# Zeros written by VectorE ten units into the third block, attention's steps queued ahead of the gates', and one routing step a unit later

## The chip, the cores and the metric

The kernel runs on one core of one Trainium2 chip. Its time is in device microseconds (us), from the first to the last work of the core; a version's time is the median of its runs. Beside the timed runs there is one profiled execution, from which all rows come.

## What is computed

Three layers follow each other. Attention works on chunks of 64 positions; its output is the input of a dense layer pair with a hard-swish-like gate; that output goes through a mixture of eight experts, of which each token uses the best two.

```python
scores = scale * np.matmul(q_c, k_c.transpose(0, 1, 2, 4, 3))
attn = softmax(scores)                       # within a chunk of 64
x = np.matmul(attn, v_c)                     # as 2304 tokens x 512
h = x @ w_in                                 # 512 -> 2048
x = (h * np.clip(h + 3.0, 0.0, 6.0) / 6.0) @ w_out
noisy_logits = x @ w_gate + np.log1p(np.exp(x @ w_noise)) * noise
top2 = np.argpartition(-noisy_logits, 2, axis=1)[:, :2]
...
out[mask] += top2_w[mask, k, None] * (np.maximum(x[mask] @ w1[e], 0.0) @ w2[e])
```

## The kernel before, in words

The 2304 tokens are 18 tiles of 128 rows, in five blocks of 4, 3, 4, 4 and 3 tiles (BT, lines 31 to 33). The dense layer runs block by block, and each block is 16 units (the 2048 inner columns by 128). A unit of `regular` (line 781) is, on TensorE: 12 matmuls into one bank (`s1`, line 297: four row pieces in three passes, since an operand is split into a high and a low fp32r part), then three matmuls for each tile of the unit before (`s2`, line 307). ScalarE and VectorE turn the bank into the next operand between them (lines 332 to 339), so TensorE is always one unit behind with the second product.

Into these units other work is woven, by `between` (line 802). Three dictionaries, A, B and Z, say what is run at which place of which unit: Z right after `mlp_s1`, A after `mlp_act`, B at the unit's end. A counter (`ticks`) puts TensorE's part between the matmuls of `s1` and `s2`. While block b is worked on:

- attention of the tiles of block b+1 is made: scores (`att_sc`, line 200, TensorE), maximum and difference (lines 207 and 213, VectorE), exponential (line 226, ScalarE), in the next unit the sums and the normalising (`att_n`, lines 231 to 238, VectorE), then transposes (line 250, TensorE), a copy (line 254, ScalarE), the product with v (line 267, TensorE) and the split of the result (lines 277 and 280). At the end the next tile of q, k and v is loaded into the freed half of `arena` (line 122, SP's queue).
- the gates of block b-1 are made. `x2_out` (line 363) stores the four finished tiles of block b-1 in DRAM (`x2d`). `gate_l` (line 383) loads a tile back with its rows turned into quarters, four small loads `xq<-x2d` on SP's queue; `gate_d` (line 375) transposes it on VectorE into `xT`; `gate_mm` (line 415, TensorE) multiplies it with the gate weights, two tiles at a time; `gate_lp`, `gate_rt` and `gate_rr` sum it up.
- `gate_top` (line 446 on) picks the two experts in four steps, `gate_pm` (line 502, TensorE) and `gate_ps` (line 518 on) find each token's slot, and `gate_ps` ends with indirect DMAs from GpSimd's queue that write the table (line 525).

TensorE, VectorE and ScalarE run exactly in the order in which the program calls these steps (`manual_schedule`). SP's and GpSimd's queues do not: a planner puts their instructions where it reckons that their operands are ready. Each engine takes its own instructions strictly one after the other, so an instruction that waits holds all behind it.

`zero_out` (line 739) fills one tile of 128x1024 with zeros (line 741) and writes it with five DMAs of 1536 KB from SP's queue over the first rows of `x2d` and over the whole output (line 745), to which the experts add later. The tile is one of three buffers that carry raw weights elsewhere.

The calls, with their numbers (unit numbers of attention; unit and tiles of a gate; unit of `gate_top`, steps of it in a unit):

```python
regular(1, {}, *between(1, (1, 4, 7, 10), ((4, 2), (8, 2)), 11, 2))
side = {}
at(side, 8, zero_out)
regular(2, side, *between(2, (1, 3, 5, 7), ((4, 2), (8, 1)), 10, 2))
```

After the fourth block the experts follow, eight units each, with gathers from `x2d`, their products and the adding scatters into the output.

Of the kernel before, what the change touches and what calls it, by code (L numbers as in the profile page):

```python
# [19 lines left out]
P = 128  # L20
NT = 2304
DM = 512
# [6 lines left out]
B0 = [sum(BT[:b]) for b in range(len(BT))]  # L29
# [23 lines left out]
def tile_kernel(ctx, tc, qkv, w1u, w2u, wg, noise, out):  # L53
    nc = tc.nc
# [8 lines left out]
    first = tc.tile_pool(name="first", bufs=1, space=PSUM)  # L63
# [13 lines left out]
    def bank(tag, shape, name):  # L77
        i, j = in_pair[tag]
        t = single[tag] if tag in single else pairs[i][:, j * DM:(j + 1) * DM]
        if len(shape) == 2:  # L80
            return t[:, :shape[1]]
        return t[:, :shape[1] * shape[2]].rearrange("p (a b) -> p a b", b=shape[2])
# [235 lines left out]
    def gtile():  # L318
        return work.tile([P, 2 * CAP], F32R, tag="g", bufs=2, name="g")


    def mlp_s1(b, u, g, off):
        n = BT[b] * P
        h = hbank(n)
        s1(h, st["w", "m", u], xb[b], 0, n)
        st["h", b] = h
        st["g", b, u] = g[:, off:off + 2 * n].rearrange("p (j n) -> p j n", j=2)

    def mlp_act(b, u):
        n = BT[b] * P  # L330
        r = work.tile([P, DM], F32, tag="r", bufs=2, name="r")[:, :n]
        nc.scalar.activation(r, st["h", b], AF.Relu, bias=b3)  # L332
        nc.vector.scalar_tensor_tensor(r, r, 6.0, st["h", b], op0=ALU.min, op1=ALU.mult)  # L333
        nc.scalar.activation(st["g", b, u][:, 0], r, AF.Copy)  # L334
        st["r", b] = r

    def mlp_lo(b, u):
        g = st["g", b, u]
        nc.vector.tensor_tensor(g[:, 1], st["r", b], g[:, 0].bitcast(F32), op=ALU.subtract)  # L339

    def mlp_o(b, u):
        if u == 0:
            st["acc", b] = [bank(ACC[i], [P, DM], "acc") for i in range(BT[b])]
        s2(st["acc", b], st.pop(("g", b, u)), st["w", "m", u], BT[b], u == 0, u == U1 - 1)


    def x2_out(b):
        extra = None
        for i in range(BT[b]):
            t = B0[b] + i  # L350
            if b == NB - 2 and i > 2:
                x2 = arena[:, i]
            elif i > 2:
                if extra is None:
                    extra = work.tile([P, 2, DM], F32, tag="raw", bufs=3, name="x2e")
                x2 = extra[:, i % 2]
            else:
                x2 = work.tile([P, DM], F32, tag="x2", bufs=3, name="x2")
            if i % 2 == 1:
                nc.vector.tensor_scalar(x2, st["acc", b][i], 1.0 / 6.0, None, op0=ALU.mult)  # L360
            else:
                nc.scalar.activation(x2, st["acc", b][i], AF.Copy, scale=1.0 / 6.0)
            nc.sync.dma_start(x2d[ND + t * P:ND + (t + 1) * P, :], x2)
            st["x2", t] = x2
# [40 lines left out]
    ENDS = [pairs[0][:, :2 * P], pairs[0][:, 6 * P:]]  # L405
# [332 lines left out]

    def zero_out():
        zero = work.tile([P, 2 * DM], F32, tag="raw", bufs=3, name="zero")  # L740
        nc.gpsimd.memset(zero, 0.0)  # L741
        for d in (x2d[:ND], out):
            d = d.rearrange("(p r) d -> p (r d)", p=P).rearrange("p (r d) -> p r d", d=2 * DM)
            for r in range(0, d.shape[1], 3):
                nc.sync.dma_start(d[:, r:r + 3], zero[:, None, :].to_broadcast([P, 3, 2 * DM]))
# [33 lines left out]
    def at(d, u, f, *a):  # L779
        d.setdefault(u, []).append((f, *a))  # L780

    def run(lst):
        for f, *a in lst:
            f(*a)
# [6 lines left out]
    def regular(b, side, A={}, B={}, Z={}):  # L791
        nonlocal prev
        for u in range(U1):
            mlp_s1(b, u, gtile(), 0)
            run(Z.get(u, []))
            mlp_act(b, u)
            run(A.get(u, []))
            for pb, v in prev:
                mlp_o(pb, v)
            mlp_lo(b, u)  # L800
            for pb, v in prev:
                if v == U1 - 1:
                    x2_out(pb)
            run(B.get(u, []))
            if b == NB - 1 and u > 0:
                pump()
            run(side.get(u, []))
            prev = [(b, u)]

    def between(b, attn, gates, top, per):  # L810


        A, B, Z, nt, n0 = {}, {}, {}, BT[b], st.get("tick", 0)
        before = BT[b - 1]

        def s2_(u, k, f, *a):
            n = n0 + 3 + k if u == 0 else n0 + 3 + before + (3 + nt) * (u - 1) + 3 + k
            at(ticks, n, f, *a)

        def s1_(u, k, f, *a):  # L820
            n = n0 + k if u == 0 else n0 + 3 + before + (3 + nt) * (u - 1) + k
            at(ticks, n, f, *a)


        first = B0[b - 1]
        for u, n in gates:
            ts = list(range(first, first + n))
            first += n
            for i, t in enumerate(ts):
                at(B, u - n - 1 + i, gate_l, t)  # L830
                at(B, u - n + i, gate_d, t)
            if nt > 3:
                s2_(u, nt, gate_mm, ts, ENDS[0])
                at(B, u, gate_lp, ts)
                s1_(u + 1, 2, gate_rt, ts, ENDS[1])
                s1_(u + 1, 2, gate_rr, ts)
            else:
                p5 = bank("p5", [P, DM], "lg")
                s1_(u + 1, 1, gate_mm, ts, p5)
                at(A, u + 1, gate_lp, ts)  # L840
                s1_(u + 2, 1, gate_rt, ts, p5[:, 2 * P:])
                s1_(u + 2, 1, gate_rr, ts)
        for i, u in enumerate(attn):
            t = B0[b + 1] + i
            if nt > 3:
                s2_(u, nt, att_sc, t, 0, outer)
            else:
                s1_(u, 2, att_sc, t, 0, outer)
            at(B, u, att_mx, t, False)
            at(B, u, att_e, t)  # L850
            at(B, u + 1, att_n, t)
            if nt > 3:
                s1_(u + 2, 3, att_pt, t)
                at(A, u + 2, att_at, t, at_[0])
                s2_(u + 2, nt, att_xo, t)
                end = (B, u + 2)
            else:
                s2_(u + 2, 1, att_pt, t)
                at(B, u + 2, att_at, t, at_[0])
                s1_(u + 3, 2, att_xo, t)  # L860
                end = (Z, u + 3)
            at(*end, att_hi, t)
            at(*end, att_lo, t)
            if t + 2 < NTILE:
                at(*end, load_tile, t + 2, bufs[4 + t % 2])
        for i in range(4):
            at(B, top + i // per, gate_top, b - 1, 1)
        pos, pm = ENDS[1] if nt > 3 else bank("p5", [P, DM], "pos"), top + 5 - per
        s2_(pm, 1, gate_pm, b - 1, pos)
        at(B, pm, gate_ps, b - 1)  # L870
        return A, B, Z
# [51 lines left out]
    def pump():  # L923

        j = nxt["u"]
        if j < U1 + NE * U2:
            split_unit(j)
            load_raw(j + 3)
            nxt["u"] = j + 1
# [24 lines left out]

    with tc.manual_schedule(engines={nc.tensor.engine, nc.vector.engine, nc.scalar.engine}):
        block0()
        regular(1, {}, *between(1, (1, 4, 7, 10), ((4, 2), (8, 2)), 11, 2))
        side = {}
        at(side, 8, zero_out)
        regular(2, side, *between(2, (1, 3, 5, 7), ((4, 2), (8, 1)), 10, 2))  # L960
        side = {}
        for j in range(3):
            at(side, 12 + j, load_raw, U1 + j)
        regular(3, side, *between(3, (1, 3, 5), ((4, 2), (8, 2)), 10, 1))
# [5 lines left out]
    side = {}  # L970
# [7 lines left out]
    for gi, (key, e, t0, nt, off) in enumerate(groups):  # L978
        side = {}
# [127 lines left out]
```

## Time and profile before

| | before |
|---|---|
| time, median of 3 runs | 949.82 us (948.93 to 951.11) |
| the profiled execution's own time | 942.81 us |
| its span, first to last instruction | 941.0 us |
| TensorE busy | 909.5 us (97%) |
| VectorE, ScalarE, GpSimd busy | 51%, 35%, 24% |
| mean granted TensorE clock | 0.991 |
| moved by DMA | 101.49 MB |

A line of the grouped view reads: line of the kernel, engine, operation, what it writes and reads, number, then busy us and mean ns, then the idle time of the engine before it and what ended that. In views in order of time the first two numbers are the start and the duration in us, and a bracket at the end gives the idle time of the engine just before and its releaser. PE is TensorE, PEld its weight load, DVE VectorE, ACT ScalarE, POOL GpSimd, SPq the queue of SP.

### The profile page before, as it was taken

The numbers are of one execution on the slowest core, as the hardware profiler recorded it, in microseconds if no ns is written. First come the engines' busy times: TensorE is split into PE (matmuls) and PEld (weight loads), VectorE is DVE, ScalarE is ACT, GpSimd is POOL, SyncE is SP. The second block draws the span as 40 slices with busy tenths as digits, with TensorE's granted clock in tenths as the row PEclk, the third lists the DMA queues.
The fourth block names the chain that finished last, engine by engine and source line by source line (L and its number), as shares of the span: only waits on it lengthen the run. The fifth ranks groups of instructions, "written<-read, shape, count | busy, mean of one in ns | idle before, by whom it ended". The sixth has DMA issues, their size and how long they took to land. (4 is left out here: it accounts for less than half of the span.)

```text
span 941.0 us, 14426 instructions
## 1 busy us (share of the span) xinstructions
PE 909.5 (97%) x5814; PEld 767.7 (82%) x5814; DVE 481.5 (51%) x907; ACT 331.5 (35%) x638; POOL 230.4 (24%) x213
## 2 busy tenths in 40 slices
PE   6999996999999999999999999999999999999996
PEld 3677785887778777888988898888898988888884
DVE  6999962554544454336553455444545544441311
ACT  5555431333332232244551443333333333321210
POOL 0000000002001000032202435753655445332311
PEclk9999997999999999999999999999999999999998
DMA  9636548113220310013640664563636455240422
GB/s 346 204 102 195 187 173 285 38 64 57 79 90 1 112 57 1 1 57 83 187 147 2 161 165 129 125 151 95 158 99 132 118 118 140 69 54 20 54 24 33
DMA packets 49916, 101.49 MB, mean 108 GB/s; under 512 B 17040, under 2 KB 23056, under 8 KB 49840
## 3 DMA queue, kind: packets, MB, share of 16 engines
q1 hardware_dynamic: 38736, 80.38, 27.4%
q0 software_dynamic: 11104, 20.10, 11.8%
q8 instruction: 47, 0.77, 0.4%
q14 instruction: 29, 0.24, 0.1%
HBM read 77.66 MB, written 22.75 MB: 107 GB/s over the span
## 5 line engine op out<-in xcount | busy, mean ns | idle before, releaser
L307 PE MATMUL bp<-w,g 128*128 128x512 f32 (+1 forms) x1812 | 451.1, 396 | 0.4 <-ACT g L334 0.3
L307 PEld LDWEIGHTS bp<-w,g 128*128 128x128 f32 (+1 forms) x1812 | 329.3, 185 | 73.9 <-DVE g L339 0.8
L297 PE MATMUL bp<-Xa,w 128*128 128x304 f32 (+3 forms) x1344 | 244.0, 332 | 2.5 <-ACT w L181 2.1
L297 PEld LDWEIGHTS bp<-Xa,w 128*128 128x128 f32 x1344 | 209.1, 188 | 30.3 <-ACT w L181 5.5
L560 POOL DMA_INDIRECT xrq<-x2d,iq x114 | 119.3, 1046 | 95.9 <-DVE iq L554 34.6
L603 DVE SCALAR_TENSOR_TENSOR g<-bp,g 128x304 fp32r<-128x304 f32 (+2 forms) x128 | 60.3, 471 | 131.0 <-ACT g L602 131.0
L142 DVE TENSOR_TENSOR w<-raw,w 128x1024 fp32r<-128x1024 f32 x64 | 78.4, 1226 | 89.3 <-ACT w L141 87.6
L525 POOL DMA_INDIRECT table<-pay,slot x36 | 36.1, 1002 | 346.6 <-DVE slot L522 245.0
L602 ACT ACTIVATE g<-bp 128x304 fp32r<-128x304 f32 (+2 forms) x128 | 54.2, 424 | 168.7 <-PE bp L297 168.5
L297 PE MATMUL bp<-Xb,w 128*128 128x384 f32 (+1 forms) x480 | 107.0, 368 | 0.0
L297 PE MATMUL bp<-Xe,w 128*128 128x304 f32 (+1 forms) x672 | 102.7, 308 | 0.0
L297 PEld LDWEIGHTS bp<-Xe,w 128*128 128x128 f32 x672 | 99.8, 188 | 3.3
L333 DVE SCALAR_TENSOR_TENSOR r<-r,bp 128x512 f32<-128x512 f32 (+1 forms) x80 | 50.6, 632 | 91.0 <-ACT r L332 90.9
L297 PEld LDWEIGHTS bp<-Xb,w 128*128 128x128 f32 x480 | 86.7, 190 | 11.8 <-issue 1.2
L630 POOL DMA_INDIRECT out_dram<-arena,tab x40 | 62.7, 1566 | 123.6 <-DVE arena L627 100.2
L141 ACT ACTIVATE w<-raw 128x1024 fp32r<-128x1024 f32 x64 | 67.7, 1058 | 59.2 <-PE bp L307 58.6
L332 ACT ACTIVATE r<-bp,b 128x512 f32<-128x512 f32 (+1 forms) x80 | 51.1, 639 | 106.0 <-PE bp L297 106.0
L334 ACT ACTIVATE g<-r 128x512 fp32r<-128x512 f32 (+1 forms) x80 | 47.2, 590 | 73.3 <-DVE r L333 73.3
L339 DVE TENSOR_TENSOR g<-r,g 128x512 fp32r<-128x512 f32 (+1 forms) x80 | 51.0, 637 | 40.2 <-ACT g L334 40.2
L181 ACT ACTIVATE w<-u 128x512 fp32r<-128x512 f32 x32 | 20.3, 633 | 32.8 <-DVE u L174 32.8
L375 DVE STREAM_TRANSPOSE arena<-xrq 128x512 f32<-128x512 f32 (+1 forms) x30 | 31.4, 1045 | 0.0
L741 POOL MEMSET zero<- 128x1024 f32 x1 | 1.0, 953 | 115.3 <-DVE u L174 115.3
(150 smaller groups left out, 478.3 us busy)
## 6 DMA issues: line engine op xcount, KB each, us to landing
raw<-in_w2u_dram SPq DMA_DIRECT2D x64, 512.0 KB
raw<-in_w1u_dram SPq DMA_DIRECT2D x24, 512.0 KB
arena<-in_qkv_dram SPq DMA_DIRECT2D x14, 768.0 KB
out_dram<-zero SPq DMA_DIRECT2D x4, 1536.0 KB
rawx<-in_w1u_dram SPq DMA_DIRECT2D x8, 512.0 KB
x2d<-x SPq DMA_DIRECT2D x15, 256.0 KB
xq<-x2d SPq DMA_DIRECT2D x44, 64.0 KB
xrq<-x2d,iq POOLq DMA_INDIRECT x114, 3.0
```

What stands on the lines that cost most here:

```text
L141: nc.scalar.activation(w[:, 0], raw, AF.Copy)
L142: nc.vector.tensor_tensor(w[:, 1], raw, w[:, 0].bitcast(F32), op=ALU.subtract)
L297: nc.tensor.matmul(dst, w[:, a, kd * P:(kd + 1) * P], x[:, b, kd, t0:t0 + n], start=(k == 0), stop=(k == 3 * KD - 1))
L307: nc.tensor.matmul(acc[i][:gi.shape[2]], gi[:, a], w[:, b, DM:], start=(first and j == 0), stop=(last and j == 2))
L332: nc.scalar.activation(r, st["h", b], AF.Relu, bias=b3)
L333: nc.vector.scalar_tensor_tensor(r, r, 6.0, st["h", b], op0=ALU.min, op1=ALU.mult)
L334: nc.scalar.activation(st["g", b, u][:, 0], r, AF.Copy)
L339: nc.vector.tensor_tensor(g[:, 1], st["r", b], g[:, 0].bitcast(F32), op=ALU.subtract)
L560: nc.gpsimd.indirect_dma_start(out=xr[:, c * P:(c + 1) * P], out_offset=None, in_=x2q, in_offset=bass.IndirectOffsetOnAxis(ap=st["iq", key ...
L602: nc.scalar.activation(g[:, 0, t0:t0 + n], h, AF.Relu)
L603: nc.vector.scalar_tensor_tensor(g[:, 1, t0:t0 + n], h, 0.0, g[:, 0, t0:t0 + n].bitcast(F32), op0=ALU.max, op1=ALU.subtract)
L630: s = nc.gpsimd.indirect_dma_start(out=out, out_offset=bass.IndirectOffsetOnAxis(ap=tab[:n, i, 0:1], axis=0), in_=y, in_offset=None, compu ...
```

## The change

Three edits.

1. `zero_out` fills its tile on VectorE in place of GpSimd, and is called at unit 10 of the third block (block index 2) in place of unit 8. VectorE keeps to the written order, so the filling now stands in the program where it is called.
2. In `between` the loop that queues attention's steps comes ahead of the loop that queues the gates', so that within a unit attention's steps are called first.
3. For the first block's gates (made during block index 1), `gate_top` starts at unit 12 in place of 11, and `gate_pm` and `gate_ps` move from unit 14 to 15.

```diff
     def zero_out():
         zero = work.tile([P, 2 * DM], F32, tag="raw", bufs=3, name="zero")
-        nc.gpsimd.memset(zero, 0.0)
+        nc.vector.memset(zero, 0.0)
...
-        first = B0[b - 1]
-        for u, n in gates:
...
         for i, u in enumerate(attn):
             t = B0[b + 1] + i
...
+        first = B0[b - 1]
+        for u, n in gates:
+            ts = list(range(first, first + n))
+            first += n
+            for i, t in enumerate(ts):
+                at(B, u - n - 1 + i, gate_l, t)
+                at(B, u - n + i, gate_d, t)
...
-        regular(1, {}, *between(1, (1, 4, 7, 10), ((4, 2), (8, 2)), 11, 2))
+        regular(1, {}, *between(1, (1, 4, 7, 10), ((4, 2), (8, 2)), 12, 2))
         side = {}
-        at(side, 8, zero_out)
+        at(side, 10, zero_out)
         regular(2, side, *between(2, (1, 3, 5, 7), ((4, 2), (8, 1)), 10, 2))
```

What it moves on the engines shows at three places. The first is SP's queue from the stores of the first block on (`x2d<-x2e` is the last of them); `xq<-x2d` are the quarter loads of the gates, four to a tile, `arena<-in_qkv_dram` the loads of q, k and v.

```order
 L363 DMA x2d<-x_1348 128x512
 L363 DMA x2d<-x2e 128x512
+L383 DMA xq<-x2d 32x4x128 x12
+L122 DMA arena<-in_qkv_dram 128x1536
 L383 DMA xq<-x2d 32x4x128 x4
-L745 DMA x2d<-zero 384x1x1024
-L745 DMA out_dram<-zero 128x3x1024 x4
-L383 DMA xq<-x2d 32x4x128 x4
-L122 DMA arena<-in_qkv_dram 128x1536
-L383 DMA xq<-x2d 32x4x128 x8
 L122 DMA arena<-in_qkv_dram 128x1536 x3
```

Before, the planner had put the zeros' five DMAs between the quarter loads of the first and of the second tile; now the loads of the first three tiles follow the stores directly. The zeros' new place on the same queue is at the end of the third block, ahead of its stores:

```order
 L122 DMA arena<-in_qkv_dram 128x1536 x3
+L745 DMA x2d<-zero 384x1x1024
+L745 DMA out_dram<-zero 128x3x1024 x4
 L135 DMA raw<-in_w2u_dram 128x1024
 L363 DMA x2d<-x_2870 128x512
```

They have moved behind the last load of q, k and v of that block, and ahead of a load of an expert's weights (line 135) and the stores of the third block. The third place is VectorE in unit 2 and 3 of block index 1, where `xT` is the gates' transpose and lines 231 to 238 are `att_n`:

```order
-L375 STREAM_TRANSPOSE xT<-xq 128x512
-L231 TENSOR_REDUCE su<-arena 128x8
-L232 TENSOR_SCALAR su<-su 128x8
-L233 RECIPROCAL su<-su 128x8
-L238 TENSOR_TENSOR arena<-arena,su 128x512
+L231 TENSOR_REDUCE su<-arena 128x8
+L232 TENSOR_SCALAR su<-su 128x8
+L233 RECIPROCAL su<-su 128x8
+L238 TENSOR_TENSOR arena<-arena,su 128x512
+L375 STREAM_TRANSPOSE xT<-xq 128x512
 L333 SCALAR_TENSOR_TENSOR r<-r,bp_427 128x384
```

The transpose has gone behind the normalising of the same unit; the same swap, or one with lines 207 and 213, stands in the other units that have both.

## Rows read from the trace of the kernel before

**Rows 1.** The page: busy us, share of the span, instructions, of TensorE.

```profile
PE 909.5 (97%) x5814; PEld 767.7 (82%) x5814; DVE 481.5 (51%) x907; ACT 331.5 (35%) x638; POOL 230.4 (24%) x213
```

**Rows 2.** TensorE's waits: what waited for what, us in total, times, longest.

```profile
PE bp L415 <- DVE xT L375: 8.8, 1, 8.8
...
PE pair L250 <- DVE arena L238: 0.8, 3, 0.4
```

**Rows 3.** SP's queue in order of time, after the first block's stores.

```profile
130.91 1.92 SPq L383 DMA_DIRECT2D xq<-x2d  x4
132.87 0.65 SPq L745 DMA_DIRECT2D x2d<-zero  x1
133.56 4.51 SPq L745 DMA_DIRECT2D out_dram<-zero  x4
138.12 9.33 SPq L383 DMA_DIRECT2D xq<-x2d  x4
```

**Rows 4.** Stretches: PE, PEld, DVE, ACT, POOL busy; granted clock; DMA share, GB/s.

```profile
133.00:140.00 7.00, 7.00 (x38) 6.38 (x37) 4.62 (x8) 2.15 (x4) 0.00 (x0) 1.00 0.94 352
...
150.00:155.00 5.00, 0.11 (x5) 0.00 (x0) 0.00 (x0) 0.00 (x0) 0.00 (x0) 0.72 1.01 332
155.00:160.00 5.00, 1.11 (x10) 0.73 (x11) 2.11 (x3) 0.10 (x1) 0.00 (x0) 0.50 0.89 232
...
162.00:163.00 1.00, 1.00 (x5) 0.87 (x4) 0.34 (x1) 0.63 (x2) 0.00 (x0) 0.80 0.28 82
```

**Rows 5.** In order of time, units 2 to 5 of block index 1: TensorE and VectorE.

```profile
138.66 1.08 DVE L375 STREAM_TRANSPOSE xT<-xq 128x512 f32<-128x512 f32 x1
...
148.89 0.86 PE L297 MATMUL bp<-Xb,w 128*128 128x384 f32 x4
149.69 0.43 PE L415 MATMUL bp<-xT,wg_sb 128*32 128x128 f32 x8
...
157.75 1.08 DVE L375 STREAM_TRANSPOSE xT<-xq 128x512 f32<-128x512 f32 x1 [14.66 <-DMA xq<-x2d]
...
158.89 0.66 PE L415 MATMUL bp<-xT,wg_sb 128*32 128x128 f32 x8 [8.78 <-DVE xT L375]
...
164.41 0.86 PE L297 MATMUL bp<-Xb,w 128*128 128x384 f32 x4
```

**Rows 6.** In order of time, TensorE in units 8 and 9 of the same block.

```profile
176.79 2.25 PE L307 MATMUL bp<-w,g 128*128 128x512 f32 x9
...
178.88 0.86 PE L297 MATMUL bp<-Xb,w 128*128 128x384 f32 x4
...
181.76 0.85 PE L307 MATMUL bp<-w,g 128*128 128x512 f32 x3
```

**Rows 7.** The page's groups: a fill, and VectorE's nearest operation on 128x1024.

```profile
L142 DVE TENSOR_TENSOR w<-raw,w 128x1024 fp32r<-128x1024 f32 x64 | 78.4, 1226 | 89.3 <-ACT w L141 87.6
...
L741 POOL MEMSET zero<- 128x1024 f32 x1 | 1.0, 953 | 115.3 <-DVE u L174 115.3
```

**Rows 8.** In order of time, VectorE at the end of unit 10, third block.

```profile
286.05 0.69 DVE L333 SCALAR_TENSOR_TENSOR r<-r,bp 128x512 f32<-128x512 f32 x1 [0.97 <-ACT r L332]
```

**Rows 9.** SP's queue from the third block's end on.

```profile
315.81 1.31 SPq L363 DMA_DIRECT2D x2d<-x  x3
...
318.29 2.09 SPq L383 DMA_DIRECT2D xq<-x2d  x4
```

**Rows 10.** A stretch of the third block, columns as in rows 4.

```profile
282.00:308.00 26.00, 26.00 (x116) 21.09 (x115) 10.19 (x38) 6.31 (x12) 5.80 (x6) 1.00 0.01 1
```

**Rows 11.** In order of time, the third block's last gate (units 7 and 8).

```profile
262.26 1.11 DVE L375 STREAM_TRANSPOSE xT<-xq 128x512 f32<-128x512 f32 x1
263.12 0.65 PE L200 MATMUL pair<-arena 64*64 64x64 f32 x32
...
269.44 0.42 PE L415 MATMUL pair<-xT,wg_sb 128*32 128x128 f32 x8
```

**Rows 12.** In order of time, the fourth block's first gate (units 3 and 4).

```profile
341.13 0.65 PE L415 MATMUL pair<-xT,wg_sb 128*32 128x128 f32 x16
```

More of the change, by code (lines that the diff above doesn't have):

```diff
@@ L822, in s1_ @@
             at(ticks, n, f, *a)
-        first = B0[b - 1]
-        for u, n in gates:
[L827 to L842, printed above, removed]
         for i, u in enumerate(attn):
@@ L865, in between @@
                 at(*end, load_tile, t + 2, bufs[4 + t % 2])
+        first = B0[b - 1]
[5 more added lines that the diff above has]
+                at(B, u - n + i, gate_d, t)
+            if nt > 3:
+                s2_(u, nt, gate_mm, ts, ENDS[0])
+                at(B, u, gate_lp, ts)
+                s1_(u + 1, 2, gate_rt, ts, ENDS[1])
+                s1_(u + 1, 2, gate_rr, ts)
+            else:
+                p5 = bank("p5", [P, DM], "lg")
+                s1_(u + 1, 1, gate_mm, ts, p5)
+                at(A, u + 1, gate_lp, ts)
+                s1_(u + 2, 1, gate_rt, ts, p5[:, 2 * P:])
+                s1_(u + 2, 1, gate_rr, ts)
         for i in range(4):
```

## The prediction

> **What bounds the kernel now.** I read the busy times first: TensorE is busy for 909.5 of 941.0 us [rows 1], so only what TensorE loses can be won, at most 31.5 us. Next TensorE's own waits, longest first: one stands out, a matmul of the gates (line 415) that waits 8.8 us, once, for a transpose on VectorE; among the rest is a group of three short waits, 0.8 us together, of attention's transposes for its normalising [rows 2]. Then I follow the long wait back. The matmul at 158.89 waited 8.78 us for the transpose, and the transpose, at 157.75, had itself waited 14.66 us for its quarter loads [rows 5]. SP's queue tells why these were late: the loads of the first tile went out at 130.91, then came the five DMAs of zeros from 132.87 on, and the loads of the second tile only began at 138.12 and took 9.33 us to be issued, behind a full queue [rows 3]. Through that time the DMA engines were busy all along: share 0.94 at 352 GB/s from 133 to 140, and still 0.89 from 155 to 160 [rows 4]. So 7.86 MB of zeros that nobody needs yet (five of 1536 KB) stand ahead of 256 KB that TensorE is about to need. Since VectorE works in order, all behind the transpose stood still too: it did nothing at all between 150 and 155 [rows 4].
>
> **What that stall costs.** The idle time is not all of it. After the pause the granted clock was 0.50, the lower level of 1.2 GHz, and came back within the stretch from 162 to 163 (0.80 there: 0.4 us at 0.50, then 1.00) [rows 4]. So TensorE worked for 162.4 - 158.89 = 3.5 us at half speed. I take both together from the length of the unit: unit 5 runs from 148.89 to the next unit's first matmuls at 164.41, 15.52 us [rows 5]. The same unit without a pause is put together from two pieces: the first product with gate matmuls in it, 181.76 - 178.88 = 2.88 us, and a plain second product, 178.88 - 176.79 = 2.09 us [rows 6], together 4.97. The stall costs 15.52 - 4.97 = 10.55 us. The Trainium skill ("TensorE: Matmul & The Clock Gate", the section on HAM oscillation) counts some 1.67 us at the low clock, half of it lost, for each pause of a kernel that it measured; as an estimate from that page the stall would be worth 8.78 + 0.84 = 9.6 us here, and the time below 0.9 us higher. The row shows 3.5 us at the low clock, and the row decides.
>
> **The change part by part.**
>
> *Zeros away from the first gate: minus 10.55 us.* Now the quarter loads of the second tile follow those of the first directly on SP's queue. They can go out at about 132.9, where the zeros went, in place of 138.12 [rows 3]. The first tile's loads, issued from 130.91 on, were there for a transpose at 138.66, 7.75 us later [rows 5], although the zeros were already being moved beside them. By the same 7.75 us from 132.9 the second tile's are there by 140.7 at the latest, and its half of the gate's matmuls comes up at about 150.1, when the first tile's eight, from 149.69, are through [rows 5]. Nothing is late next in this unit: the load of q, k and v behind these loads waits, as before, for TensorE's product of unit 4, and is used three units on.
>
> *The fill on VectorE: 0.* The trace has no fill on VectorE. From below, GpSimd's fill of the same tile took 0.95 us; from above, VectorE's subtraction on as many elements, which reads two operands, took 1.23 [rows 7]; I take 1.2, the nearer by engine. It stands behind the last search of unit 10 in the third block, and there VectorE sat idle for 0.97 us before its next instruction, waiting for ScalarE [rows 8]. So 0.2 to 0.3 us of it stick out, and delay an operand that TensorE uses one unit later, some 6 us on. If that cover were gone, it would cost 1.2 us once. The compiled order shows no wait on the fill, so VectorE cannot get stuck on it.
>
> *The zeros at their new place: 0.* They leave when the fill is done, at about 286.3 on the clock of before. There the DMA engines are idle: share 0.01, 1 GB/s, from 282 to 308 [rows 10]. 7.86 MB at 352 GB/s are 22.3 us, to 308.6; taken the other way, the old place needed at most 157.75 - 132.87 = 24.9 us for the zeros and the loads behind them, to 311.2. The next in the queue is a load of expert weights that is not used before the fifth block, and then come the stores of the third block at 315.81 [rows 9]. So 4.6 us are left. GpSimd's six scatters into the table in that stretch [rows 10] share the DMA engines with the zeros; nobody reads the table before the experts.
>
> *Attention ahead of the gates: minus 0.8 us.* The three waits of line 250 for line 238 come from a transpose of 1.1 us that stood ahead of the normalising in the same unit; it now stands behind, and all 0.8 us [rows 2] should go. In return the gates' transposes come later. The tightest is the last one in the third block: it ran at 262.26, now it comes behind the maximum and the difference (0.69 us each), which wait for scores made from 263.12 to 263.77, so it ends at about 266.3; its matmul is at 269.44 [rows 11]. 3.1 us are left, and the same count leaves about as much at the other gates. Cost 0.
>
> *Routing a unit later: 0.* The first block's scatters into the table come one unit later; what follows on GpSimd's queue is the next block's scatters, a block on (the six of [rows 10]), and the table is read by the experts alone. TensorE gets two small matmuls in another unit, none more.
>
> *The sum.* 10.55 + 0.8 = 11.35 us. The profiled execution took 942.81 us with a span of 941.0, and would take 931.5 with a span of about 929.7. The timed runs' median, 949.82, is 7.0 us above the profiled time; I let that difference stand and predict 949.82 - 11.35 = 938.5 us. A measurement of this kernel can tell about 0.2%, 1.9 us, from no change.
>
> **The rivals.**
>
> *The first gate is still late.* The tile goes out to DRAM and comes back in small pieces, and that way alone might be too long for the second tile. For it: both stores and loads are issued only as the unit runs. Against it: the first tile made the trip in time beside the zeros, and in the later blocks, which have much the same distance and no zeros, there is not one such wait: the 8.8 us were a single one [rows 2]. If half of the stall stayed, the time would be 938.5 + 5.3 = 943.8.
>
> *The zeros hold up another gate.* The fourth block's first gate needs the third block's tiles, stored from 315.81 on and loaded back from 318.29 [rows 9], on the same queue as the zeros. The Trainium skill ("DMA: Bandwidth & Descriptors", the section on queues, rings and completion order) says that each DMA engine takes a queue's descriptors in ring order; by that rule stores behind the zeros cannot pass them. The trace agrees at the old place, where loads begun at 138.12 gave no data before 157.75. From the first store to a transposed second tile take some 12 us (2.5 to the first loads; twice 2.1 to issue two tiles' loads and as much for a load of weights between them [rows 9]; 2 as a guess for the landing; 1.08 for the transpose), and the matmul is at 341.13 [rows 12]; so the zeros begin to hurt if they are not out by about 329. A fresh stall of the old size, the clock's part included, gives 949.0, no change. Slower than before by over 0.2% needs a loss above 11.35 + 1.9 = 13.3 us, thus zeros that end after 342 (329 + 13.3): 56 us for 7.86 MB, 140 GB/s against 352 [rows 4]. That would be 952 us or more. What speaks for it is only that the margin of 4.6 us to the stores is small; a transfer a few us too long is still covered by the 13 us behind it.
>
> *Late transposes.* If the moved transposes miss their matmuls, each miss costs its lateness, and VectorE's queue holds the next operand too. It decides once a transpose comes more than 3.1 us later than I reckon. With 2 us lost at each of two gates: 942.5.
>
> That the change doesn't do what it says can be left out: the order of the queue has the zeros at the new place.
>
> **How the numbers follow.** The forecast gets 0.84, the late first gate 0.05, late transposes 0.03, the zeros at their new place 0.08, half of it with no change and half slower. So faster by over 0.2%: 0.84 + 0.05 + 0.03 = 0.92; within 0.2%: 0.04; slower: 0.04. The range: if only the idle time came back, 949.82 - 8.78 = 941.0; with part of a stall left, up to 943. Downward, the timed runs are 7.0 us longer than the profiled one, and if half of that lay in the stretch that DMA bounds, the gain would be 3.5 us larger, 935. So 935 to 943.
>
> **What would show it.** Right: no wait of line 415 for line 375; a granted clock of 1.00 through 150 to 163; unit 5 of block index 1 in about 5.0 us; quarter loads on SP's queue from about 130.9 to 135 without a break; the DMA engines full from about 275 to 298 on the new clock, with TensorE busy throughout; line 250's waits for line 238 gone. Wrong: a wait of line 415 anywhere, above all near 330; VectorE waiting for quarter loads in the fourth block; any low clock between 130 and 820.

## The result, and the profile after

The changed kernel took 938.23 us (median of 4 runs, 937.79 to 938.40); the kernel before, beside it on the same chip, 949.38 us (4 runs, 948.28 to 951.11). The ratio is 0.988 (95% interval 0.9863 to 0.9897): 11.2 us faster, where 11.35 were forecast.

The profiled execution took 937.79 us with a span of 936.0, against 942.81 and 941.0 before. So the two profiles differ by 5.0 us only, the timed runs by 11.2. Why, is the first thing to settle; ahead of it stand the lines that answer to those of before. The page's busy times of the changed kernel, then the longest of TensorE's waits:

```profile
PE 910.3 (97%) x5814; PEld 767.9 (82%) x5814; DVE 482.9 (52%) x908; ACT 331.7 (35%) x638; POOL 230.6 (25%) x212
```

```profile
PE bp L297 <- DVE g L603: 3.9, 2, 2.0
```

Both waits of [rows 2] are gone: line 415 waits nowhere for line 375, and the three waits of line 250 for `arena` are not there either. VectorE has one instruction more, GpSimd one less: the fill. At the head of the list stands a wait that the kernel before did not have, 3.9 us for line 603, which is an expert's. SP's queue from the first block's stores on, VectorE's transposes of the first two tiles, and two stretches (columns as in [rows 4]):

```profile
128.21 1.32 SPq L363 DMA_DIRECT2D x2d<-x  x3
...
130.32 3.90 SPq L383 DMA_DIRECT2D xq<-x2d  x8
```

```profile
139.87 1.10 DVE L375 STREAM_TRANSPOSE xT<-xq 128x512 f32<-128x512 f32 x1
142.47 1.08 DVE L375 STREAM_TRANSPOSE xT<-xq 128x512 f32<-128x512 f32 x1
```

```profile
150.00:155.00 5.00, 5.00 (x28) 4.56 (x27) 2.82 (x7) 1.61 (x4) 0.00 (x0) 1.00 0.18 52
155.00:160.00 5.00, 5.00 (x87) 4.31 (x85) 2.28 (x4) 1.59 (x3) 0.00 (x0) 1.00 0.00 0
```

Where TensorE worked for 0.11 of 5 us and the DMA engines were full [rows 4], it is now busy throughout at a granted clock of 1.00 (the upper level, 2.4 GHz), and the DMA engines are nearly idle (shares 0.18 and 0.00). The eight quarter loads of the first two tiles go out without a break, in 3.90 us, and the second tile's transpose starts at 142.47, where it started at 157.75 before [rows 5]. In order of time on TensorE, the unit that held the stall [rows 5]:

```profile
147.73 0.86 PE L297 MATMUL bp<-Xb,w 128*128 128x384 f32 x4
148.53 0.64 PE L415 MATMUL bp<-xT,wg_sb 128*32 128x128 f32 x16
...
152.71 0.86 PE L297 MATMUL bp<-Xb,w 128*128 128x384 f32 x4
```

All sixteen matmuls of the gate come in one piece, 5 us after the end of the second transpose, and the unit lasts 152.71 - 147.73 = 4.98 us in place of 15.52. To see what the whole did, I take the length of the stages from SP's queue, from the first store of one block's tiles to that of the next. From block index 0's stores to block index 3's the kernel before took 412.82 - 128.78 = 284.04 us, the changed one 400.24 - 128.21 = 272.03: 12.0 us less. Behind that, among the experts, the profile of the changed kernel loses 7.6 us again (block index 3's stores come 412.82 - 400.24 = 12.6 us earlier, the end of the span only 5.0). In order of time on TensorE, in the units of the second expert, and the last ScalarE operation ahead of the gap's end:

```profile
556.43 3.63 PE L307 MATMUL bp<-w,g 128*128 128x512 f32 x15
561.95 1.52 PE L297 MATMUL bp<-Xe,w 128*128 128x304 f32 x9 [1.89 <-DVE g L603]
563.76 0.69 PE L297 MATMUL bp<-Xe,w 128*128 128x304 f32 x2 [0.28 <-issue]
565.17 0.41 PE L297 MATMUL bp<-Xe,w 128*128 128x304 f32 x1 [0.72 <-issue]
567.61 3.38 PE L297 MATMUL bp<-Xe,w 128*128 128x304 f32 x12 [2.02 <-DVE g L603]
570.81 3.65 PE L307 MATMUL bp<-w,g 128*128 128x512 f32 x15
```

```profile
566.62 0.42 ACT L602 ACTIVATE g<-bp 128x304 fp32r<-128x304 f32 x1 [5.24 <-PE bp L297]
```

From one second product to the next (556.43 to 570.81) are 14.38 us, against 6.83 in the units around it. The waiting matmuls name VectorE, and ScalarE's operation of line 602 started late too, but TensorE also stops for "issue" between matmuls of one product, so it is no late operand alone. The granted clock fell to 0.50 there, from 564 to 569. The change touches nothing there. The experiments took this up.

### The profile page after: what moved, and what is told of

It reads as the page before. It is cut to its first block, busy times and chain, and to the rows that moved or that the text cites. A ratio compares the mean times of both kernels' runs of the same rounds, so it can differ in the third digit from the quotient of the medians.

```text
span 936.0 us, 14421 instructions
## 1 busy us (share of the span) xinstructions
PE 910.3 (97%) x5814; PEld 767.9 (82%) x5814; DVE 482.9 (52%) x908; ACT 331.7 (35%) x638; POOL 230.6 (25%) x212
## 4 chain that ended last, share of the span: by engine, by line
PE 86%; DVE 10%; ACT 2%; issue 1%; DMA 0%; POOL 0%; SPq 0%; POOLq 0%; ACTq 0%
PE bp L307 41%; PE bp L297 41%; DVE u L174 2%; DVE u L166 2%; DVE u L165 1%; DVE r L333 1%; DVE w L188 1%; DVE g L339 1%; PE pair L267 1%; PE pair L200 1%; ACT w L181 1%; PE pair L250 1%; PE bp L587 1%; DVE mx L207 0%; PE bp L399 0%
## 5 line engine op out<-in xcount | busy, mean ns | idle before, releaser
L297 PE MATMUL bp<-Xe,w 128*128 128x304 f32 (+1 forms) x672 | 105.1, 311 | 4.9 <-DVE g L603 3.9
L188 DVE TENSOR_TENSOR w<-u,w 128x512 fp32r<-128x512 f32 x32 | 22.0, 688 | 2.7 <-ACT w L181 1.5
```

Of the source, the lines that this page charges most:

```text
L297: nc.tensor.matmul(dst, w[:, a, kd * P:(kd + 1) * P], x[:, b, kd, t0:t0 + n], start=(k == 0), stop=(k == 3 * KD - 1))
```

## The experiments

They ran on three chips: sections 1 and 2 on the first, 3 to 6 on the second, 7 on the third. The kernel before was timed beside them on each: 942.17 us (19 runs, 940.76 to 944.15), 950.24 (19 runs, 947.64 to 954.40) and 950.24 (one run). Differences of times below are between runs on one chip.

**1. The two kernels again.** No edit in either.

> The kernel before, unchanged, for a second profile. Theory A (the changed kernel gained its 11 us at the first gate, and the pause of some 6 us among the experts that its profile shows belongs to most executions of either kernel and only missed the one profile of before): the wait of line 415 is there again, 8 to 10 us, and this profile also has TensorE idle for some 5 us between 540 and 620, with a span near 947. Theory B (the pause came with the change): the wait is there, no such pause among the experts, span near 941. Ratio 1.000 by both.

> The changed kernel, unchanged. Theory A: ratio 0.988, no wait of line 415; the pause among the experts is there or not, and wherever it is absent the span is about 930. Theory B: ratio 0.988, the pause is there every time, span 936.

The kernel before: 942.03 us, ratio 0.9996 (0.9987 to 1.0005), span 939.2. The changed one: 928.83 us (928.61 to 929.08), ratio 0.9859 (0.9843 to 0.9874), span 926.8, near the 929.7 forecast. In neither is there a long unit among the experts: the kernels are 7 and 9 us faster than on the first occasion, and the gain is 13.3 us. Taken alone, the profile of the kernel before looks like theory B, for which the pause came with the change; the changed kernel's profile speaks against that, since it has no pause either. TensorE's waits of the kernel before, this time:

```profile
PE bp L415 <- DVE xT L375: 8.3, 1, 8.3
...
PE pair L267 <- ACT at L254: 1.1, 2, 0.6
```

The stall is 8.3 us, not 8.8: it varies between executions. The times of the kernel before vary by 3.4 us on this chip (19 runs), the changed kernel's by 0.5 (4 runs); that the stall makes the difference isn't shown. The wait of line 267, of TensorE's product with v for a copy on ScalarE, has the same numbers in the first profile of the kernel before, and I had not read it.

**2. One part at a time.** The first run has the zeros alone, against the kernel before:

```diff
-        nc.gpsimd.memset(zero, 0.0)
+        nc.vector.memset(zero, 0.0)
...
-        at(side, 8, zero_out)
+        at(side, 10, zero_out)
```

> Only the zeros moved (VectorE, unit 10 of the third block); order within the units and routing as before. Forecast: 10.55 us of the gain, so about 938.9 where before is 949.4, ratio 0.989; the three waits of line 250 for line 238 stay (0.8 us). Rival (the order within the units matters more, since VectorE no longer has attention's work behind a waiting transpose): the gain stays under 8 us, above 941, and a wait for a transpose or a normalising shows in its place.

931.06 us (930.63 to 932.14), ratio 0.9884 (0.9869 to 0.9899): 11.1 us, above the 8 us that the rival allowed. Block index 1, from store to store, lasts 79.06 us; it was 89.60 in the first profile of the kernel before (218.38 - 128.78) and 89.07 in its second, the one on this chip. The stall was thus worth 10.54 and 10.0 us; the forecast had 10.55. The stores on SP's queue, in the first profile of the kernel before and in this run:

```profile
128.78 1.32 SPq L363 DMA_DIRECT2D x2d<-x  x3
...
218.38 1.31 SPq L363 DMA_DIRECT2D x2d<-x  x3
```

```profile
128.08 1.31 SPq L363 DMA_DIRECT2D x2d<-x  x3
...
207.14 1.31 SPq L363 DMA_DIRECT2D x2d<-x  x3
```

TensorE's waits keep the two others:

```profile
PE pair L267 <- ACT at L254: 1.1, 2, 0.6
...
PE pair L250 <- DVE arena L238: 0.8, 3, 0.4
```

The second run has the rest alone, the new order of the loops in `between` (the diff ahead of the prediction) and the routing step:

```diff
-        regular(1, {}, *between(1, (1, 4, 7, 10), ((4, 2), (8, 2)), 11, 2))
+        regular(1, {}, *between(1, (1, 4, 7, 10), ((4, 2), (8, 2)), 12, 2))
```

> Attention's steps ahead of the gates' and routing a unit later, with the zeros as before. Forecast: 0.8 us, about 948.6, ratio 0.999; the wait of line 415 stays at 8 to 10 us. Rival: the order takes a good part of the stall away, since attention's normalising no longer stands behind the late transpose: under 946, ratio below 0.996.

939.82 us (938.58 to 942.60), ratio 0.9976 (0.9965 to 0.9987): 2.35 us, by the interval 1.2 to 3.3. Its longest wait is still the gate's, 8.8 us.

The parts add up: 11.1 + 2.35 = 13.45 against 13.3 for both. But 2.35 is three times the 0.8 of the forecast, and all of the interval is above it. Placing the trace with the zeros alone beside the whole change, matmul by matmul, the difference arises at five places on TensorE: four transposes of attention (line 250) gain 0.58, 0.38, 0.34 and 0.50 us, and one product with v (line 267) 0.51, together 2.31. Between the first profile of the kernel before and this run's, the same five places gain 0.59, 0.38, 0.33, 0.51 and 0.52. Of the four transposes the first, the second and the fourth have a wait row, of 0.35, 0.17 and 0.28 us. So each of these was worth some 0.2 us more than the idle time that the view of waits puts down to it, and the third stands in no wait row at all. The row of line 267 has 0.45 at its place, near the 0.51 gained.

**3. Which part moves line 267.** The zeros as above, and the routing step a unit later, in the old order of the loops.

```diff
-        regular(1, {}, *between(1, (1, 4, 7, 10), ((4, 2), (8, 2)), 11, 2))
+        regular(1, {}, *between(1, (1, 4, 7, 10), ((4, 2), (8, 2)), 12, 2))
```

> Zeros moved and the first block's routing a unit later; the order within the units as before. Theory (the routing takes the wait of line 267 for the copy on ScalarE away in block index 1, since two routing steps no longer stand on ScalarE ahead of it): 0.5 us under the kernel with the zeros alone (0.9884 of before), ratio 0.9878, and line 267's waits fall from 1.1 to 0.6 us in the profile while line 250's 0.8 stay. Rival (that 0.5 us comes from the order within the units too): no gain over the kernel with the zeros alone, line 267's waits unchanged.

```profile
PE pair L267 <- ACT at L254: 0.6, 1, 0.6
PE pair L250 <- DVE arena L238: 1.4, 3, 0.8
```

One of the two waits of line 267 is gone, and those of line 250 are still three. Block index 1 lasts 78.57 us in place of 79.06. So the routing step is worth 0.49 us in these two profiles. The way to it is longer than the expectation has it. In order of time in unit 12, on VectorE and ScalarE, first with the zeros alone, then in this run (the two profiles' times differ by 0.07 us up to there):

```profile
187.91 0.54 DVE L333 SCALAR_TENSOR_TENSOR r<-r,bp 128x384 f32<-128x384 f32 x1
188.48 0.52 ACT L334 ACTIVATE g<-r 128x384 fp32r<-128x384 f32 x1 [2.19 <-DVE r L333]
188.91 0.58 ACT L254 ACTIVATE at<-pair 128x512 f32<-128x512 f32 x1
```

```profile
185.82 0.56 DVE L333 SCALAR_TENSOR_TENSOR r<-r,bp 128x384 f32<-128x384 f32 x1 [0.69 <-ACT r L332]
186.84 0.58 ACT L254 ACTIVATE at<-pair 128x512 f32<-128x512 f32 x1
```

The two operations of `gate_top` on ScalarE (lines 457 and 458) made line 332 only 0.45 us later. Most of the 2.0 us by which the copy of line 254 was later, of which TensorE lost 0.5, came from VectorE: `gate_top`'s operations of lines 460 to 467, the search for the two experts among them, stood there ahead of line 333, ScalarE's line 334 waited 2.19 us for that, and the copy stands behind line 334. The sum of line 250's waits is larger here because one of them is 0.75 us where it was 0.17; just ahead of it this profile has a short pause (last section). The time, 940.08 us with a ratio of 0.9889 (0.9862 to 0.9916), can't tell half a microsecond.

**4. The whole change on the second chip.** No edit.

> The changed kernel for a third profile. Its first profile had one unit of the second expert at 14.38 us in place of 6.83, its second profile none. Theory (the pause belongs to the chip or the execution and not to the kernel): either no such unit and a span near 927, or one again, and then the kernel before has a time near 949 beside it. Rival (it belongs to the changed kernel, in some executions): such a unit while the kernel before stays at 942.

937.92 us (935.94 to 942.97), ratio 0.9853 (0.9825 to 0.9882). The long unit is back: 17.37 us in place of 6.83, and in the other three profiles on this chip 12 to 14 us. The kernel before ran 8 us slower beside them than on the first chip, as the theory had it. The ratio of the change is alike on three occasions: 0.988, 0.9859, 0.9853.

**5. How much cover the fill has.** Nine fills of the tile in place of one.

```diff
-        nc.vector.memset(zero, 0.0)
+        for _ in range(9):
+            nc.vector.memset(zero, 0.0)
```

> The changed kernel with the zeros' tile filled nine times over on VectorE in place of once: eight fills more of 0.91 us, 7.3 us, at the end of unit 10. In the second profile of the changed kernel the operand behind the fill is done at 275.4 and its product begins at 277.9, so 2.5 us are free. Theory (the fill is hidden by a unit's distance): the first 2.5 us cost nothing and the rest stops TensorE, 4.8 us more than the changed kernel (5 to 6 with a lower clock). Rival 1 (VectorE's time there is on the path): 7.3 us more. Rival 2 (the distance is larger than that): 0 to 1 us more.

946.72 us (944.36 to 948.64), 8.8 us above the whole change beside it. That is more than the 5 to 6 of the theory, and the time alone is nearest to the first rival (7.3 us, VectorE's time all on the path). In order of time the last fill and what follows on ScalarE and TensorE, then the stretch behind it:

```profile
282.95 0.91 DVE L742 MEMSET zero<- 128x1024 f32 x1 [0.28 <-DVE zero L742]
...
284.44 0.63 ACT L334 ACTIVATE g<-r 128x512 fp32r<-128x512 f32 x1 [10.25 <-DVE r L333]
...
285.12 5.49 PE L307 MATMUL bp<-w,g 128*128 128x512 f32 x12 [6.14 <-ACT g L334]
```

```profile
284.00:288.00 4.00, 2.88 (x7) 2.25 (x8) 2.79 (x15) 1.41 (x3) 0.00 (x0) 0.50 0.73 280
```

A fill takes 0.91 us and the next starts 1.19 us after its start, so eight more are 9.5 us, not the 7.3 expected. TensorE waited for 6.1 of them: 3.4 us are covered, and the rival that put all of it on the path is out. Then TensorE worked at the lower level, 0.50 or 1.2 GHz; twelve matmuls took 5.49 us, in place of 2.95 for twelve at the upper. Block index 2 is 9.2 us longer than that of the whole change beside it (107.09 against 97.88): 6.1 of wait and 3.1 at the lower clock. One fill is hidden altogether. In the second profile of the change, in order of time on VectorE:

```profile
272.55 0.91 DVE L741 MEMSET zero<- 128x1024 f32 x1 [0.16 <-issue]
273.38 0.66 DVE L333 SCALAR_TENSOR_TENSOR r<-r,bp 128x512 f32<-128x512 f32 x1
```

Line 333 follows on the heels of the fill, and the view of TensorE's waits has no row of that unit.

**6. The zeros five units later**, so that the transfer meets the stores of the third block.

```diff
-        at(side, 10, zero_out)
+        at(side, 15, zero_out)
```

> The changed kernel with the zeros called at unit 15 of the third block in place of unit 10, five units (some 27.6 us) later. SP's order is the same, the zeros now go out at about 301 and end at about 324, where the stores of the third block stand behind them from 303. Theory (the place of the zeros is all, and a stall comes wherever a gate's tiles are behind them): the fourth block's first gate (its matmul at 328) waits for its second tile, which needs some 12 us from the first store on; so 324 + 12 - 328 = 8 us of wait and 1.8 us for the clock, about 9 to 10 us more than the changed kernel, and the wait shows in line 415 for line 375. Rival (what hurt at the old place was the short way of the first gate, and a later place is harmless): within 1 us of the changed kernel.

950.97 us (947.15 to 953.49), ratio 1.0004 (0.9984 to 1.0023): the whole gain is lost, 13.0 us more than the change beside it. SP's queue in this run, then what waited, in order of time:

```profile
299.91 0.65 SPq L745 DMA_DIRECT2D x2d<-zero  x1
...
309.60 5.00 SPq L363 DMA_DIRECT2D x2d<-x  x3
...
325.50 1.75 SPq L383 DMA_DIRECT2D xq<-x2d  x4
```

```profile
330.49 1.08 DVE L375 STREAM_TRANSPOSE xT<-xq 128x512 f32<-128x512 f32 x1 [12.31 <-DMA raw<-in_w2u_dram]
331.49 0.65 DVE L333 SCALAR_TENSOR_TENSOR r<-r,bp 128x512 f32<-128x512 f32 x1
...
333.34 1.13 PE L267 MATMUL pair<-at,arena 64*64 64x64 f32 x32 [10.99 <-ACT at L254]
```

The stores go out from 309.60 and the loads that need them only from 325.50, 15.9 us later, where 2.48 us lay between them before (315.81 to 318.29 [rows 9]). It is a stall of the same kind as the one removed, but by another road. The gate's matmul did not wait: the transpose of the *first* tile held VectorE for 12.3 us, behind it stood line 333 of the dense layer, behind that ScalarE's lines 334 and 254, the copy for attention, and TensorE stopped at line 267. The view names a load of weights from the same queue as the transpose's releaser; the transpose reads `xq` alone, whose loads left from 325.50, so they are the likelier cause. The stretches show the granted clock at 0.50 from 326 to 338:

```profile
326.00:330.00 4.00, 0.00 (x0) 0.00 (x0) 0.00 (x0) 0.00 (x0) 0.00 (x0) 0.50 0.81 264
330.00:335.00 5.00, 1.66 (x61) 1.66 (x64) 2.35 (x3) 1.11 (x2) 0.00 (x0) 0.50 0.32 66
335.00:338.00 3.00, 3.00 (x20) 2.30 (x16) 1.94 (x4) 0.60 (x1) 0.00 (x0) 0.50 0.80 257
```

From the second block's stores to the fourth's are 207.36 us, against 194.05 in the whole change: 13.3 us. The expectation had the stall some 3 us smaller, the size of the old one, and at line 415.

**7. The kernel before on a third chip**, for the long unit.

> The kernel before once more, for the long unit of the second expert alone, which the profile of the kernel before never showed while its times beside the paused kernels stood some 8 us higher. If the pause belongs to the chip and the hour, this profile shows that unit either at 6.8 us with a time near 942 us, or at 12 to 17 us with a time near 950 us, and nothing between. If the pause belongs to the changed kernel alone, the unit is at 6.8 us whatever the time. The stall of TensorE at the first gate of the third block is 8 to 9 us either way.

948.76 us, span 947.0. TensorE in order of time, and the last gather of a row on GpSimd:

```profile
568.08 3.63 PE L307 MATMUL bp<-w,g 128*128 128x512 f32 x15
...
579.00 3.25 PE L297 MATMUL bp<-Xe,w 128*128 128x304 f32 x12 [3.52 <-DVE g L603]
582.08 3.63 PE L307 MATMUL bp<-w,g 128*128 128x512 f32 x15
```

```profile
575.01 0.94 POOL L560 DMA_INDIRECT xrq<-x2d,iq  x1 [0.30 <-issue]
```

The unit lasts 14.00 us (568.08 to 582.08) in the kernel before too. So the pause is no part of the change. The stall of line 415 is 8.7 us, at its old place in block index 1 (not the third block, as the expectation says). The pause comes late in a nearly unbroken row of gathers on GpSimd (line 560), one each 1.25 us, and ends some 3 us after that row. But the same row of gathers stands in the profiles on the first chip, without a pause. What makes it is open; nothing was run to find out.

## Why the prediction was right, point by point

- **Zeros away from the first gate, minus 10.55 us: right, and the mechanism too.** The store-to-store lengths give 10.54 and 10.0, and the timed runs of the zeros alone 11.1. The unit lasts 4.98 us, for 4.97 reckoned, the two tiles' loads go out in one row, and the clock stays at 1.00. By the Trainium skill's count ("TensorE: Matmul & The Clock Gate", on HAM oscillation) the stall would, as an estimate, have been worth 9.6. The lengths are all above it, and so the measured length of the unit was the better price.
- **The fill, 0: right.** It takes 0.91 us, for 1.2 estimated, below even GpSimd's 0.95 [rows 7]. The cover was put at 0.97 us of idle time ahead of line 333 [rows 8], with an operand behind it that TensorE uses some 6 us on. Nine fills take 10.4 us (eight times 1.19 and 0.91) and stopped TensorE for 6.1: the whole cover is 4.3 us, more than the first and less than the two together.
- **The zeros at their new place, 0: right.** In the second profile they leave at 273.49 with a load of weights behind them, and the DMA engines are full until about 297:

```profile
273.49 0.65 SPq L745 DMA_DIRECT2D x2d<-zero  x1
...
278.72 5.25 SPq L135 DMA_DIRECT2D raw<-in_w2u_dram  x1
303.10 1.31 SPq L363 DMA_DIRECT2D x2d<-x  x3
```

```profile
292.00:296.00 4.00, 4.00 (x19) 3.29 (x18) 0.56 (x2) 0.69 (x1) 2.29 (x3) 1.00 1.01 292
296.00:300.00 4.00, 4.00 (x18) 3.21 (x18) 1.02 (x2) 0.63 (x1) 0.00 (x0) 1.00 0.30 87
```

  About 24 us, the load of weights included, within the 22.3 to 24.9 reckoned, and some 6 us ahead of the stores.
- **The order within a unit, minus 0.8, and the routing, 0: the size failed.** Together they gave 2.3 us (2.35 timed). The step that failed is the pricing of the order by the sum of the three wait rows: it gave 1.8 us, since each place was worth some 0.2 us more and a fourth has no row. For the routing I looked at GpSimd's queue and at TensorE's two matmuls, and not at what its steps hold up on VectorE and ScalarE: a wait row of line 267 stood in the kernel before, and 0.5 us was to be had. No transpose came late.
- **The rival of another gate: rightly a rival, wrongly bounded.** I took the matmul at 341.13 [rows 12] for the deadline and gave the zeros until about 329. The run at unit 15 shows that the deadline is VectorE's arrival at the first tile's transpose; in the change it stands 13.9 us behind the stores (303.10, 317.02):

```profile
317.02 1.09 DVE L375 STREAM_TRANSPOSE xT<-xq 128x512 f32<-128x512 f32 x1
```

  On the clock of before that is 329.7. From the stores to the loads are 2.5 us, and in the run at unit 15 from the loads to the transpose 5.0 (325.50, 330.49), so zeros hurt from about 322 on: 6 us of cover lay behind the margin of 4.6, not 13. That run bears out the sum, though the 5.0 are its own: zeros from 299.91 on, 23.7 us long as in the second profile of the change (273.49 to some 297.2), and 7.5 for the tile's way give 331.1, and the transpose began at 330.49. And such a stall costs 13 us, not the 10.5 of the old one. The trace agrees with the rule of ring order that I quoted from the Trainium skill ("DMA: Bandwidth & Descriptors", queues, rings and completion order): the loads that need the stores behind the zeros could go out only 15.9 us after them (309.60 to 325.50).
- **The profiled span, 929.7: 926.8 in the profile without the pause, 936.0 in the first.** I let the 7.0 us between the timed runs and the profile of before stand, and that was right for the time; but its likely place, among the experts, was not seen. The lower end of the range supposed a half of it in the stretch that the DMA bounds, and no run shows any of it there: the profile on the third chip, with a time of 948.76, has 284.00 us from block index 0's stores to block index 3's, where the first had 284.04. A sign that the prediction named as wrong did come up, a low clock between 130 and 820 (0.50 from 564 to 569); it belongs to the pause among the experts, which the kernel before has too. That 938.5 came within 0.3 us of 938.23 is partly luck: the gain was 11.2 us on that occasion, 13.3 and 12.3 on the two others.

## What to carry to other kernels

A bulk transfer that nobody needs yet belongs where its queue has a gap as long as itself, and its deadline is not the matmul that uses the next data: it is the first instruction, on any engine that works in order, that waits for them, with all that is queued behind it. Pin such a transfer by an instruction on an engine whose order you write yourself: with the fill left on GpSimd, the compiled order has the zeros at the old place even when they are called two units later. That program was compiled only; no run takes the fill's engine and the place of the call apart. And price a swap in the order by the start times of the matmuls in both traces; the rows of waits showed less than half of this one.

## What was not expected of the hardware

- A pause of 5 to 11 us in one unit of the second expert, in six of eleven profiles, of the kernel before and of changed ones: in all five on the second and third chip, in none of the four on the first. The same six profiles, and no other, have shorter stops elsewhere, where the releaser is given as "remote". In five of them, all of changed kernels, one stands at the start of block index 2, here in the run of section 3:

```profile
214.39 1.53 PE L297 MATMUL bp<-Xa,w 128*128 128x512 f32 x6 [0.66 <-issue]
...
214.62 0.69 DVE L207 TENSOR_REDUCE mx<-pair 128x8 f32<-128x512 f32 x1 [2.98 <-remote]
```

  That the 7 us between the first profile of the kernel before and its timed runs are this pause is likely: the profile on the third chip, which has it, is 6.0 us longer in span than the first, and on the first chip, without it, profile and timed runs of the kernel before are 1 us apart. But timed runs leave no trace, so it isn't shown.
- A fill of 128x1024 f32 takes 0.91 us on VectorE and 0.95 on GpSimd, but on VectorE 1.19 from one to the next.
- After a wait of 6.1 us TensorE worked on at 0.50 until about 291, some 6 us, and after one of 11.0 us until after 338, some 5 us: about half of that is added to the price of the wait.
